# Four early x loads, single-tile norms, more warm-up products and one last FFN group of four tiles

## The chip, the cores and the metric

The kernel runs on one core of one Trainium2 chip. The metric is the device time of one execution in microseconds. A core has five instruction queues that matter here: TensorE (PE, with its weight loads, PEld), VectorE (DVE), ScalarE (ACT), GpSimd (POOL) and SyncE (SP), which issues nearly all DMAs. Each runs its own list of instructions in order and waits on semaphores for the others.

## The reference

One transformer block with adaptive layer norm, on x of 2048 x 512 in bf16. A vector c gives, through silu and w_mod, six vectors of 512: shift, scale and gate for each half.

```
mod = silu(c) @ w_mod                      # 6 x 512: sa, ca, ga, sb, cb, gb
h = layernorm(x) * (1 + ca) + sa
q, k, v = split(h @ wqkv)                  # 32 heads of 16
logits[s, w] = q[s] . k[s - 2w] / 4        # w = 0..7, masked where s - 2w < 0
o[s] = sum_w softmax(logits)[s, w] * v[s - 2w]
x = x + ga * (o @ wo)
h = layernorm(x) * (1 + cb) + sb
x = x + gb * ((silu(h @ w1) * (h @ w3)) @ w2)   # inner width 1792
```

## The kernel before

The 2048 rows are 16 tiles of 128. All weights and x stay in SBUF once they are loaded. The work has three stages, and the stages of different tiles overlap.

**First norm and q, k, v.** `LN1` groups the tiles as 0-1, 2-3, 4-7, 8-11, 12-15. `ln_stats` (line 576) computes mean and variance on DVE, adds epsilon, raises to the power -1/2 on POOL, and normalizes on DVE (tile 0 on ACT). It takes one tile at a time in the first group and pairs in the others; for tiles 0 and 1 the epsilon is added on DVE, else on POOL. `ln_T` (line 644) brings h into feature-major form: PE transposes with an eviction on ACT that also applies scale and shift, or, for the groups that `DMA_T` names, DMA transposes followed by ACT. `proj_qk` and `proj_v` are PE products; ACT evicts them, and v is stored to a scratch in DRAM by SP (line 764), from which `values` later loads shifted windows of 1 MB. Three buffers hold v between eviction and store, so an eviction of v waits until an earlier store has landed.

**Attention.** `BLOCKS` takes pairs of tiles. The products of q with eight shifted k are DVE instructions of 128 x 4096 (`pq`, line 781), summed per head by PE (line 791). Softmax runs on DVE and ACT. DVE multiplies the weights into the loaded windows of v (line 868 and 873), PE adds them up (line 886), ACT evicts, a DMA transpose on SP turns the result (`ot`, line 893), PE multiplies by wo (line 901), and DVE adds the residual (line 906).

**FFN.** `FFN` groups the tiles. `ln_sums` (line 613) is the second norm, on ACT and POOL. For each of 14 slices of the inner width `ffn_unit` (line 911) makes a product with w1 (silu on ACT), one with w3, and their product on DVE (line 933); products have 256 or 512 columns by the group's size. `ffn_w2` (line 940) multiplies by w2 per tile in two halves of seven slices; tiles 14 and 15 go in column halves (line 950). A group's units may start only as slices of the group before are read, since 20 buffers serve 14 slices.

**The start.** `rows` gives the layout in which x is read (the attention uses two orders of rows). Tiles 0 to 7 go to a borrowed buffer (`sb_pq`) for the first norm and are loaded a second time, later, into `x_sb`. SP issues the loads in order: x of tile 0, of tile 1, the first 1 MB of w_mod (`wm_s`, line 451), and then slices of wqkv and x. Until w_mod has landed, PE runs `NWARM` warm-up products of 256 columns (line 545), the small product that transposes c, and the transposes of tile 0. Then follow the modulation products (line 531), the modulated h on DVE and ACT, and the first q and k products (line 728).

**The order.** Nothing is scheduled at run time: `ORDER` lists all operations by their number in the order of construction, and each engine's queue is that list cut down to its own operations (`place`, line 143). `SLOTS` gives the buffer of every pooled value. `synchronize` (line 165) puts a wait where a value or a buffer comes from another engine. So every queue, the one of SP with its DMAs too, is fixed and blocks at its head.

Of the kernel before, what the change touches and what calls it, by code (L numbers as in the profile page):

```python
# [264 lines left out]
FFN = [[0,1],[2,3],[4,5,6,7],[8,9,10,11],[12,13],[14,15]]  # L265
BLOCKS = [[[0, 1]], [[2, 3]], [[4, 5]], [[6, 7]], [[8, 9]], [[10, 11]], [[12, 13], [14, 15]]]
NWARM = 25
NATL = (0, 1, 2, 3, 6, 7)
NAT = (6, 7)
TURN_DMA = (4,5,6,7)  # L270
UPA = {}
DMA_T = ((3, 4), (2, 3, 4, 5))
# [3 lines left out]
def _build(p, A_x, A_wqkv, A_wo, B_w1, B_w3, B_w2, c, w_mod, out):  # L276
# [176 lines left out]
    load_x(2, 4, 30)  # L453
# [122 lines left out]
    def ln_stats(Ts):  # L576
# [10 lines left out]
        if i < 2:  # L587
            o = p.op("dve", lambda e: e.tensor_scalar(rsn, mv[:, i:i + n, 1], EPS, None, op0=ALU.add), 65, k, r=vms, w=[va])
            if i == 0:
                vneg = Val("nmean0")  # L590
                p.op("pool", lambda e: e.tensor_scalar(nb[:, 0:1, 0], mv[:, 0:1, 0], -1.0, None, op0=ALU.mult), 210, k, r=vms, w=[vneg])
        else:
            o = p.op("pool", lambda e: e.tensor_tensor(rsn, mv[:, i:i + n, 1], bass.AP(cst, 0, [[2, P], [0, n]]), ALU.add), 210, k,
                     r=vms + [vcst], w=[va])
# [46 lines left out]
    def pairs(Ts):  # L641
        return [Ts[i:i + 2] for i in range(0, len(Ts), 2)]
# [336 lines left out]
    for gi, Ts in enumerate(LN1):  # L979
        vns = [v for pr in ([[T] for T in Ts] if gi == 0 else pairs(Ts)) for v in ln_stats(pr)]  # L980
# [153 lines left out]
```

## Time and profile before

| what | value |
|---|---|
| time, median of 3 runs | 238.24 us (237.93 to 238.61) |
| the profiled execution | 237.94 us, its span 236.2 us |
| PE busy | 229.8 us, 97% |
| DVE busy | 178.8 us, 76% |
| ACT busy | 147.7 us, 63% |
| POOL busy | 20.0 us, 8% |
| granted TensorE clock | 0.999 |
| DMA moved | 40.42 MB, mean 171 GB/s |

The profile shows one execution from its first to its last instruction. Matmuls are pipelined, so a product's length is not its step; the distance between two starts is. Some records of products are missing. DMA issues on SP appear with the time that SP needs to issue them; the transfer itself ends later, when it lands.

### The profile page before, as it was taken

The page shows a single profiled execution, that of the slowest core. Times are in us where ns is not written, and L with a number is a line of the kernel's source. Part 1 is how long each engine was busy: PE and PEld are TensorE (multiplying, and loading weights), DVE is VectorE, ACT ScalarE, POOL GpSimd, SP SyncE. Part 2 cuts the span into 40 slices and gives each one's busy share as a digit, 9 for nine tenths or more (in the row PEclk, how much of TensorE's full clock was granted, in tenths as well). Part 3 has the DMA queues.
Part 4 walks back from the last instruction along what each step waited for, and adds up shares of the span by engine and source line. Part 5 has one row for each costly group of instructions (what it writes and reads, how often), then busy time and mean ns, then how long its engine had stood idle before and what let it go on. Part 6 is the DMA issues. An engine that isn't in the chain of part 4 may idle for free.

```text
span 236.2 us, 4478 instructions
## 1 busy us (share of the span) xinstructions
PE 229.8 (97%) x1768; PEld 136.0 (58%) x1794; DVE 178.8 (76%) x286; ACT 147.7 (63%) x298; POOL 20.0 (8%) x44
## 2 busy tenths in 40 slices
PE   7999999999999999999999999999999999999995
PEld 5766554544597586564444444444465457485774
DVE  5598999999979999999999999793364403434433
ACT  3299587979989855985746786829866415040300
POOL 5432050002000000110001010001010000000000
PEclk9999999999999999999999999999999999999999
DMA  6999589999999783896591854441311000000202
GB/s 198 391 324 311 140 305 236 220 261 369 359 264 405 280 263 100 255 263 217 147 293 54 305 139 69 86 180 44 76 38 44 25 0 1 0 25 0 71 0 89
DMA packets 42717, 40.42 MB, mean 171 GB/s; under 512 B 23224, under 2 KB 39624, under 8 KB 40648
## 3 DMA queue, kind: packets, MB, share of 16 engines
q1 hardware_dynamic: 42688, 40.14, 57.4%
q8 instruction: 14, 0.23, 0.4%
q14 instruction: 7, 0.06, 0.1%
q10 hardware_dynamic: 8, 0.00, 0.0%
HBM read 30.67 MB, written 4.21 MB: 148 GB/s over the span
## 4 chain that ended last, share of the span: by engine, by line
PE 87%; DMA 4%; ACT 4%; DVE 1%; issue 1%; SPq 1%; POOL 0%; ACTq 0%
PE pall L918 41%; PE pall L962 18%; PE pall L728 7%; PE pall L901 5%; PE pall L750 4%; PE pall L886 3%; PE pall L791 3%; PE pall L950 3%; DMA sb_wm_s<-in_w_mod_dram 2%; DMA v_scratch_dram<-sb_v 2%; PE pall L671 1%; SPq L124 1%; ACT sb_xn L636 1%; ACT sb_xn L621 1%; ACT sb_q L739 1%
## 5 line engine op out<-in xcount | busy, mean ns | idle before, releaser
L918 PE MATMUL pall<-sb_h,sb_w 128*128 128x256 bf16 (+1 forms) x664 | 101.1, 307 | 0.6 <-ACT sb_ac L892 0.2
L918 PEld LDWEIGHTS pall<-sb_h,sb_w 128*128 128x128 bf16 x672 | 65.0, 98 | 35.8 <-issue 1.1
L933 DVE TENSOR_TENSOR sb_hh<-sb_sg,pall 128x256 bf16<-128x256 bf16 (+1 forms) x84 | 39.9, 506 | 36.7 <-PE pall L918 31.2
L924 ACT ACTIVATE sb_sg<-pall 128x256 bf16<-128x256 f32 (+1 forms) x84 | 36.0, 452 | 45.3 <-PE pall L918 41.9
L962 PE MATMUL pall<-sb_w,sb_hh 128*128 128x512 bf16 x190 | 44.0, 379 | 0.3
L781 DVE TENSOR_TENSOR sb_pq<-sb_q,sb_kT 128x4096 bf16<-128x4096 bf16 x16 | 36.4, 2285 | 0.0
L962 PEld LDWEIGHTS pall<-sb_w,sb_hh 128*128 128x128 bf16 x196 | 18.9, 98 | 21.7 <-issue 0.4
L728 PE MATMUL pall<-sb_h,sb_wqkv 128*128 128x512 bf16 (+1 forms) x156 | 30.3, 335 | 0.7 <-issue 0.4
L728 PEld LDWEIGHTS pall<-sb_h,sb_wqkv 128*128 128x128 bf16 x160 | 14.7, 98 | 11.9 <-ACT sb_v L760 0.8
L972 DVE TENSOR_TENSOR sb_o<-pall,sb_x 128x512 bf16<-128x512 f32 (+1 forms) x18 | 11.1, 628 | 9.7 <-PE pall L962 6.0
L629 POOL TENSOR_TENSOR sb_rs<-sb_rs,sb_cst 128x2 f32<-128x2 f32 x8 | 6.8, 855 | 135.4 <-ACT sb_rs L627 135.4
L656 ACT ACTIVATE sb_h<-sb_h,sb_modc 128x512 bf16<-128x512 bf16 (+1 forms) x24 | 16.3, 733 | 3.0 <-DMA sb_h<-sb_xn 3.0
L868 DVE TENSOR_TENSOR sb_vsh<-sb_vsh,sb_al 128x4096 bf16<-128x4096 bf16 x7 | 15.9, 2287 | 0.0
L750 PE MATMUL pall<-sb_wqkv,sb_h 128*128 128x512 bf16 x60 | 15.2, 379 | 0.3 <-issue 0.2
L901 PE MATMUL pall<-sb_wo,sb_ot 128*128 128x512 bf16 x60 | 14.7, 379 | 0.3 <-issue 0.2
L873 DVE TENSOR_TENSOR sb_vsh<-sb_vsh,sb_al 128x2048 bf16<-128x2048 bf16 x12 | 14.3, 1222 | 0.3 <-DMA sb_vsh<-v_scratch_dram 0.2
L892 ACT ACTIVATE sb_ac<-pall 128x512 bf16<-128x512 f32 x16 | 9.6, 604 | 5.7 <-PE pall L886 5.6
L679 ACT ACTIVATE sb_h<-pall,sb_modc 128x256 bf16<-128x256 bf16 (+1 forms) x18 | 9.8, 614 | 4.7 <-DVE sb_modc L536 3.8
L636 ACT ACTIVATE sb_xn<-sb_x,sb_nb,sb_rs 128x512 bf16<-128x512 bf16 x16 | 12.6, 807 | 0.1
L906 DVE SCALAR_TENSOR_TENSOR sb_x<-pall,sb_x 128x512 bf16<-128x512 f32 x16 | 10.9, 687 | 1.6 <-PE pall L901 1.5
L621 ACT ACTIVATE sb_xn<-sb_x,sb_nm 128x512 bf16<-128x512 bf16 x16 | 11.4, 715 | 0.2
L740 ACT ACTIVATE sb_kT<-pall 128x512 bf16<-128x512 f32 x16 | 9.4, 604 | 3.1 <-PE pall L728 3.1
(94 smaller groups left out, 212.7 us busy)
## 6 DMA issues: line engine op xcount, KB each, us to landing
sb_vsh<-v_scratch_dram SPq DMA_DIRECT2D x13, 1024.0 KB, 7.2
sb_w<-in_B_w_dram SPq DMA_DIRECT2D x6, 512.0 KB, 6.6
sb_vshx<-v_scratch_dram SPq DMA_DIRECT2D x3, 1024.0 KB, 6.5
sb_w<-in_B_w_dram SPq DMA_DIRECT2D x6, 384.0 KB, 6.3
sb_x<-in_A_x_dram SPq DMA_DIRECT2D x8, 256.0 KB, 6.9
v_scratch_dram<-sb_v SPq DMA_DIRECT2D x16, 128.0 KB, 6.2
out_dram<-sb_o SPq DMA_DIRECT2D x14, 128.0 KB, 2.3
sb_wqkv<-in_A_wqkv_dram SPq DMA_DIRECT2D x6, 256.0 KB, 6.3
```

The costliest lines, as they stand in the source:

```text
L636: p.op("act", lambda e, vn=vn, T=T: e.activation(vn.at[:], x_sb[:, T, :], ACT.Identity, bias=nb[:, T, :], scale=rs[:, NT + T, :]), c_act(5 ...
L656: return e.activation(vh.at[:, ft, 0:n * P], vh.at[:, ft, 0:n * P], ACT.Identity, bias=modc[:, 8 * which + ft:8 * which + ft + 1], scale=m ...
L728: ins = e.matmul(bank(vp)[:, j * n:(j + 1) * n], wqkv[:, t, col:col + P], vh.at[:, t, 0:n], start=(t == ORDER[0] and j == 0), stop=(t == O ...
L750: ins = e.matmul(bank(vp), vh.at[:, t, tt * P:(tt + 1) * P], wqkv[:, t, 2 * D:3 * D], start=(t == ORDER[0]), stop=(t == ORDER[-1]))
L781: return e.tensor_tensor(vp.at[:], in0, in1, ALU.mult)
L868: return e.tensor_tensor(v_w, v_w, a_w, ALU.mult)
L873: return e.tensor_tensor(v_w, v_w, a_w, ALU.mult)
L901: ins = e.matmul(bank(vy), bass.AP(vt.at, ft * 2 * P + a, [[KT * 2 * P, P], [step_, P]]), wo[:, ft, :], start=(ft == 0), stop=(ft == KT - 1))
L918: ins = e.matmul(bank(vp)[:, 0:n], wt[:, t, fi * P:(fi + 1) * P], vh.at[:, t, 0:n], start=(t == 0), stop=(t == KT - 1))
L924: p.op("act", lambda e: e.activation(vt.at[:, 0:n], bank(vgp)[:, 0:n], ACT.Silu), c_act(n), k, r=[vgp], w=[vt], table="silu")
L933: p.op("dve", lambda e: e.tensor_tensor(vh_.at[:, 0:n], vt.at[:, 0:n], bank(vup)[:, 0:n], ALU.mult), c_dve(n), k, r=[vt, vup], w=[vh_])
L962: ins = e.matmul(bank(vz), vhh[fi].at[:, tt * P:(tt + 1) * P], w2[:, fi, :], start=(fi == 0), stop=(fi == NF - 1))
```

## The change

Four things are edited in the source.

- x of tiles 2 and 3 is loaded by two loads of 128 KB in place of one of 256 KB.
- `ln_stats` takes tiles 2 and 3 one at a time too, and adds epsilon for them on DVE.
- `NWARM` is 30 in place of 25.
- The last two FFN groups, tiles 12-13 and 14-15, become one of four tiles. Its transposes stay DMA transposes, and tiles 14 and 15 keep their column halves of w2.

All operations are renumbered, and `ORDER` and `SLOTS` are new. Read as queues, the new order differs as follows.

- SP: the loads of x go out as tile 2, 3, 0, 1, all ahead of w_mod's first part; the slices of wqkv follow without x between the first and the second. The second load of x2 and x3 comes right behind that of x14 and x15, ahead of the first store of v (before: behind the second pair of 1 MB windows). That of x4 and x5 comes ahead of the small store of zeros (before: behind the transposes of tiles 8 to 11). That of x6 and x7 comes behind the first slice of w1 (before: behind the first transpose of tile 10). One half of the second part of w_mod comes behind the transposes of tiles 8 to 11 (before: ahead of the first store of v). The transposes of tiles 12 to 15 go out ahead of the store of tile 4's v and of a part of wo, and not behind them.
- DVE: statistics of tiles 2 and 3 come ahead of those of 0 and 1; tiles 2 and 3 are normalized right behind the first h. The columns of both gates are cast one behind the other, ahead of tile 10's normalization (before: the second one behind tile 8's).
- POOL: the long select for the mask comes behind the powers of tiles 8 to 11 (before: ahead of those of 2 and 3).
- PE: 27 warm products ahead of tile 0's transposes and three behind them. Among the transposes of tiles 4 to 7, v of tile 3 stands behind the first two of the pair of feature blocks that ACT evicts first, and that pair goes ahead of the other. The first gate's products come between the two last q products of tiles 2 and 3, the second gate's right behind them. From there on the order is nearly the same up to the last wo product; then the units of tiles 8 to 11 are finished in order, and those of tiles 12 to 15 follow, six units, the first half of w2 of tiles 8 to 11, seven units, the second half, one unit, and then w2 of tiles 12 to 15.
- ACT: k of tiles 12 to 15, its first block, is evicted ahead of the first sums of the second norm (before: behind them). The silus of the last two groups follow PE's order, with the four modulations of tiles 12 to 15 ahead of three of them.

```diff
-FFN = [[0,1],[2,3],[4,5,6,7],[8,9,10,11],[12,13],[14,15]]
+FFN = [[0, 1], [2, 3], [4, 5, 6, 7], [8, 9, 10, 11], [12, 13, 14, 15]]
-NWARM = 25
+NWARM = 30
-DMA_T = ((3, 4), (2, 3, 4, 5))
+DMA_T = ((3, 4), (2, 3, 4))
...
     p.dma(wm_s[0][:], wm_view[:, :, 0:1024], ("load", 2), (512, 2048), w=[vwms[0]])
     load_wqk(0)
-    load_x(2, 4, 30)
+    for T in range(2, 4):
+        p.dma(x_in(T), rows(x2d, T, plain=NATL), ("load", 31 + T), (128, 1024), r=x_hold if T in early else [], w=[vxl[T]])
     load_wqk(1)
...
-        if i < 2:
+        if i < 4:
             o = p.op("dve", lambda e: e.tensor_scalar(rsn, mv[:, i:i + n, 1], EPS, None, op0=ALU.add), 65, k, r=vms, w=[va])
...
-        vns = [v for pr in ([[T] for T in Ts] if gi == 0 else pairs(Ts)) for v in ln_stats(pr)]
+        vns = [v for pr in ([[T] for T in Ts] if gi < 2 else pairs(Ts)) for v in ln_stats(pr)]
...
 ORDER = [
-    21, 20, 8, 0, 9, 18, 66, 22, 10, 11, 3, 67, 12, 4, 1, 68, 13, 23, 19, 69, 2, 70, 16, 24, 17, 71, 5, 72, 6, 62, 75,
+    25, 20, 8, 0, 9, 18, 67, 26, 10, 11, 3, 68, 12, 4, 1, 69, 13, 21, 19, 70, 2, 71, 16, 22, 17, 72, 5, 73, 6, 63, 23,
...
```

More of the change, by code (lines that the diff above doesn't have):

```diff
@@ L262, in c_dve @@
     return 60 + n * 137 // 128
-FFN = [[0,1],[2,3],[4,5,6,7],[8,9,10,11],[12,13],[14,15]]
+FFN = [[0, 1], [2, 3], [4, 5, 6, 7], [8, 9, 10, 11], [12, 13, 14, 15]]
 BLOCKS = [[[0, 1]], [[2, 3]], [[4, 5]], [[6, 7]], [[8, 9]], [[10, 11]], [[12, 13], [14, 15]]]
-NWARM = 25
+NWARM = 30
 NATL = (0, 1, 2, 3, 6, 7)
 NAT = (6, 7)
-TURN_DMA = (4,5,6,7)
+TURN_DMA = (4, 5, 6, 7)
 UPA = {}
-DMA_T = ((3, 4), (2, 3, 4, 5))
+DMA_T = ((3, 4), (2, 3, 4))
 LN1 = [[0, 1], [2, 3], [4, 5, 6, 7], [8, 9, 10, 11], [12, 13, 14, 15]]
```

131 rows, old and new, of tables (ORDER, SLOTS) are left out of this document.

## The prediction

> **What bounds the kernel now.** I read the page first, then the chain of waits, then busy time by stretch, then the timeline of single engines around each edit.
>
> ```profile
> span 236.2 us, 4478 instructions
> PE 229.8 (97%) x1768; PEld 136.0 (58%) x1794; DVE 178.8 (76%) x286; ACT 147.7 (63%) x298; POOL 20.0 (8%) x44
> PE 87%; DMA 4%; ACT 4%; DVE 1%; issue 1%; SPq 1%; POOL 0%; ACTq 0%
> ...
> 1.69 5.80 DMA sb_wm_s<-in_w_mod_dram
> ...
> 47.14 4.26 DMA v_scratch_dram<-sb_v
> 51.42 0.60 ACT sb_v L760
> ...
> 136.02 6.04 PE pall L918 x28
> ...
> 206.52 6.11 PE pall L918 x56
> ```
>
> The last rows are pieces of the chain: start, length, what. The kernel is one long PE queue. Only two things stand ahead of it or in it: the first load of w_mod, which lands at 1.69 + 5.80 = 7.49, and a detour between 47 and 59, where a store of v, an ACT eviction and the second layer norm of tiles 0 and 1 decide. The price of a step on PE is read here too: 6.11 / 56 = 0.109 us for 256 columns, 6.04 / 28 = 0.216 for 512.
>
> ```profile
> 21.50:67.00 45.50, 44.42 (x410) 23.36 (x415) 44.51 (x51) 38.31 (x76) 4.85 (x5) 1.00 0.97 270
> 68.50:151.50 83.00, 82.15 (x640) 46.73 (x649) 81.71 (x114) 61.50 (x125) 3.85 (x5) 1.00 0.68 210
> ```
>
> Columns: stretch, length, busy PE, PEld, DVE, ACT, POOL, granted clock, DMA share, GB/s. From 21.5 to 67 DVE is busy 44.5 of 45.5 us and the DMA engines 0.97. PE runs level with a full DVE and a full DMA queue there; whatever starts DVE or SP later in that stretch can reach PE.
>
> **The start: two more loads ahead of w_mod.**
>
> ```profile
> 0.78 0.86 SPq L124 DMA_DIRECT2D sb_pq<-in_A_x_dram  x2
> ...
> 1.24 2.31 PE L545 MATMUL pall<-sb_ones 128*128 128x256 bf16 x10 [1.24 <-DVE sb_ones L387]
> ...
> 3.21 0.68 DVE L582 BATCH_NORM_STATS2 sb_st<-sb_pq 128x6 f32<-128x512 bf16 x1
> ...
> 6.13 0.36 PEld L671 LDWEIGHTS pall<-sb_ident,sb_xn 128*128 128x128 bf16 x4 [0.28 <-ACT sb_xn L603]
> ...
> 6.55 0.74 PE L545 MATMUL pall<-sb_ones 128*128 128x256 bf16 x3
> ...
> 8.60 3.39 PE L728 MATMUL pall<-sb_h,sb_wqkv 128*128 128x256 bf16 x28
> ...
> 12.35 0.34 PEld L671 LDWEIGHTS pall<-sb_ident,sb_xn 128*128 128x128 bf16 x6 [0.21 <-DVE sb_xn L607]
> ...
> 2.00:3.00 1.00, 1.00 (x7) 0.67 (x5) 0.00 (x0) 0.96 (x2) 0.86 (x6) 1.00 1.02 243
> 5.00:7.50 2.50, 2.30 (x14) 1.33 (x11) 0.79 (x3) 0.81 (x1) 2.17 (x4) 1.00 1.05 389
> ```
>
> SP puts out a load every 0.45 us (1.69 - 0.78, over two), so two more move w_mod's issue by 0.9. The 262 KB ahead of it cost 262 / 389 = 0.67 at the later rate and 262 / 243 = 1.08 at the rate of the first loads. I take 0.9, ends 0.67 and 1.08: the row of 2.00 to 3.00 is that of the same kind of load, but the issue is the slower of the two only up to 0.9. [...] The q and k weights behind it wait less: the load of x2 and x3 that stood between the first and the second of them is gone, which returns 0.67.
>
> Five more warm products fill 1.05 us: ten of them take 2.31, of which the last one's 0.42 of pipeline is not a step, so a step is 1.89 / 9 = 0.21. Tile 0 is now normalized third: two statistics go ahead of it, so it starts at 3.21 + 2 x 0.68 = 4.6 instead of 3.21, its chain of 2.9 us to PE (3.21 to 6.13) and two small DVE instructions (0.2) end at 7.8, and four transposes and three products later it is about 8.4, when w_mod lands. So this hides exactly; if tile 0 is 0.2 later, PE is too (the upper end holds it).
>
> What it buys: x2 and x3 are normalized before w_mod lands. PE's q and k products then no longer wait for weights (28 of them span 3.39 - 0.27 = 3.12 from first to last start, where 27 steps of 0.109 are 2.94: 0.17 lost) nor for tile 3 (0.20 at 12.35). PE gets **+0.9 - 0.37 = +0.53**, ends 0.3 and 0.7. One POOL instruction moves too: the 1.5 us select behind the powers of tiles 10 and 11, and POOL is busy for 20 of 236 us. POOL's and DVE's one-tile additions and powers (0.15 and 0.57 each) lie in their idle time there, and so does the split into two loads.
>
> **The order at 17 to 23.**
>
> ```profile
> 17.29 0.94 PE L671 MATMUL pall<-sb_ident,sb_xn 128*128 128x128 bf16 x14
> ...
> 18.29 0.81 PE L750 MATMUL pall<-sb_wqkv,sb_h 128*128 128x512 bf16 x3
> ...
> 18.27 2.79 ACT L679 ACTIVATE sb_h<-pall,sb_modc 128x512 bf16<-128x512 bf16 x4 [0.19 <-PE pall L671]
> 20.99 1.08 ACT L739 ACTIVATE sb_q<-pall 128x512 bf16<-128x512 f32 x2
> 21.37 0.16 DVE L564 CAST sb_gcol<-pall 128x4 bf16<-128x4 f32 x1 [0.70 <-PE pall L558]
> 22.16 2.28 DVE L781 TENSOR_TENSOR sb_pq<-sb_q,sb_kT 128x4096 bf16<-128x4096 bf16 x1
> ```
>
> The new order puts tile 3's v product (four steps, 0.86) between the transposes of tiles 4 to 7 whose evictions head ACT's queue. These transposes end at 19.1 instead of 18.1: 0.53 of PE's shift, and 0.86 less the three transposes (0.33) that now come after. ACT evicts h four times (2.79) and then q twice (1.08), so q of tiles 2 and 3 is out at 23.1 and DVE's first big product starts 1.0 later. DVE agrees on its own: the second gate's column is now cast right behind the first, and waits for 16 more products behind q; tile 10's normalization, which follows it, is 0.9 late. DVE has no hole from there to 67, so all of it moves by 1.0.
>
> **SP's queue.** It is in order, and from 23 to 53 it always has something ready. Of the reloads of x (0.6 of issue each), that of tiles 2 and 3 moves ahead of the first store of v and that of 6 and 7 behind w1, so one less stands between tile 10's transposes and ot.
>
> ```profile
> 31.96 1.12 SPq L124 DMA_DIRECT2D v_scratch_dram<-sb_v  x2
> 33.12 0.60 SPq L124 DMA_DIRECT2D sb_wo<-in_A_wo_dram  x1
> 33.77 7.56 SPq L124 DMA_TRANSPOSE sb_h<-sb_xn  x4
> ...
> 43.94 2.53 SPq L124 DMA_TRANSPOSE sb_ot<-sb_ac  x2
> ...
> 33.38 0.32 DVE L607 TENSOR_SCALAR sb_xn<-sb_x,sb_mv,sb_rs 128x512 bf16<-128x512 bf16 x1
> ...
> 48.19 1.89 PE L901 MATMUL pall<-sb_wo,sb_ot 128*128 128x512 bf16 x8
> DMA to landing us min/median/max: 2.7/3.1/3.4
> ```
>
> The transposes of tiles 12 to 15 go out at 33.77, just as tile 15 is normalized (33.38 + 0.32). In the new order a store of v and a load of wo, 1.1 us of issue, come behind these transposes instead of ahead. SP will stand at them from about 33.0 (before: 33.77, less the two issues, plus 0.4 from the same lateness of DVE at tile 8), until DVE delivers tile 15 at 33.70 + 1.0. So they start 0.9 later than now, and 1.1 of issue is still to be done after them. Queued behind are ot of tile 0 and 1, then w3 and the store of v that the chain goes through at 47.14. The second ot goes out at 45.2 now and lands 2.7 later, at 47.9; PE's first wo product follows at once (48.19, of which one step is not recorded). There is no slack: PE would come 0.9 + 1.1 = 2.0 late. Against it: the four transposes took 7.56 where the two of ot took 2.53, so 2.5 us is back-pressure of a full DMA queue, and 1.7 us of silence ahead of them drains some. If all that is given back, the queue is early and PE keeps its own 0.53. Between 0.53 and 2.0 I take **1.2**: the nearest row, the 7.56, stood behind the same two megabyte loads that still stand there. It takes the place of the 0.53, and does not add to it.
>
> **From 49 to 59 PE loses time already.**
>
> ```profile
> 49.92 1.89 PE L728 MATMUL pall<-sb_h,sb_wqkv 128*128 128x512 bf16 x8
> 52.08 2.76 PE L728 MATMUL pall<-sb_h,sb_wqkv 128*128 128x512 bf16 x12 [0.27 <-ACT sb_v L760]
> ...
> 58.35 0.89 PE L671 MATMUL pall<-sb_ident,sb_xn 128*128 128x128 bf16 x8
> 59.44 0.81 PE L728 MATMUL pall<-sb_h,sb_wqkv 128*128 128x512 bf16 x3 [0.20 <-issue]
> ```
>
> Eight steps from 49.92 end at 51.65, the next starts at 52.08: 0.43. Eight transposes (0.44) and one unrecorded product (0.22) from 58.35 end at 59.0, the next starts at 59.44: 0.43. Together 0.86. They could absorb a late PE, but the store of v that they wait for is behind the same queue and moves with it, so I count nothing. From 67 on, DVE's hole of 1.5 us between the two stretches above takes in its own lateness, and PE carries its 1.2 to the end.
>
> **The last four tiles as one group.** The 224 steps of 256 columns become 112 of 512: 224 x 0.109 - 112 x 0.216 = **-0.27**.
>
> ```profile
> L933 DVE TENSOR_TENSOR sb_hh<-sb_sg,pall 128x512 bf16<-128x512 bf16 x28 | 18.5, 682 | 9.1 <-PE pall L918 7.7 <-ACT sb_sg L924 1.3
> L924 ACT ACTIVATE sb_sg<-pall 128x512 bf16<-128x512 f32 x28 | 16.0, 593 | 11.5 <-PE pall L918 8.7 <-DVE sb_hh L933 2.8
> ...
> 171.98 0.20 ACT L617 ACTIVATE sb_nm<-sb_sx 128x2 f32<-128x2 f32 x1 [1.55 <-DVE sb_x L906]
> DMA to landing us min/median/max: 2.3/2.4/2.4
> ```
>
> The first two rows are groups of equal instructions: ACT needs 0.59 and DVE 0.68 for a unit of 512 columns, PE 8 x 0.216 = 1.73, so both stay covered. The group now waits for tiles 14 and 15. From the end of the last wo product at 171.2 PE has 16 half units of the group before, 13.8 us, until 185.0. The norm starts at 171.98; its ACT queue holds a silu that needs PE's seventh half unit (177.3), so the last tile is normalized at 178.8, its transpose lands 2.4 later, and four modulations, about as long as the four evictions of 2.79 above, end at 184.1. It hides by 0.9; if that cover goes, PE waits for the difference.
>
> **The sum**: +1.2 - 0.27 = +0.9 on the profiled execution, whose own time is 237.94 (236.2 and 1.7 around it). The three runs shown have 237.93 to 238.61, median 238.24; the profiled one is 0.3 below, so I forecast 237.94 + 0.9 + 0.3, **239.1**.
>
> **Rivals.** (1) SP's queue catches up: the drained DMA queue returns the back-pressure, ot lands in time, the store of v too. PE then has +0.53, some of it absorbed in the 0.86, and -0.27: from 237.6 to 238.5. For it: 7.56 against 2 x 2.53. Against: the two loads of 1 MB are still in front. It decides once the four transposes take under 6.1 us (1.5 of the 2.0 given back). (2) Faster: w_mod is only 0.67 late, PE's 0.3 is absorbed, both losses of 0.43 vanish because w3 and the store get ahead, and the merge pays: 0.3 - 0.86 - 0.27 = -0.8, 237.4. It decides only if v's store leaves SP before 46.7. (3) The merged group's norm comes late, by a further 1 us when the last transposes wait for stores ahead of them: 240.1. (4) The clock: warm products step 0.21, the q products from 8.60 on 0.109. PE now has a hole of some 0.6 us before tile 0's transposes; the slow steps lasted from 1.24 past 6.55, over 5.3 us; if that had to be served once more from tile 0's transposes at 7.8 on, q and k would run at half speed from 9.5 to 13.1 and cost 1.8: 240.3 and more. Against it: the wait of 0.3 for w_mod at 7.2 left the clock alone. [...]
>
> **Chances.** Forecast 0.50 (238.7 to 239.9 by its own ends), rival 1 0.30, rival 2 0.12, rival 3 0.05, rival 4 0.03. What can be told from no change is about 0.3%, 0.7 us. Below 237.5 lie rival 2 and the edge of rival 1, 0.13; above 238.95 four fifths of the forecast and rivals 3 and 4, 0.48; between them 0.39. The range 237.6 to 240.1 leaves out most of rival 2 and the tops of 3 and 4.
>
> **What would show it.** w_mod lands at 8.4 and the first q product starts at 9.5; the wait on tile 3's norm is gone; DVE's first 4096-wide product starts at 23.2; SP idles before the transposes of tiles 12 to 15; wo's first product comes at 49.4; the last group's units step 0.216 with no hole ahead of them. I am wrong if wo starts before 48.6 or if the losses at 52 and 59 are gone.

## The result and the profile after

| | before | after |
|---|---|---|
| median of 15 runs each | 238.61 us (237.23 to 240.92) | 241.73 us (239.15 to 243.24) |
| ratio after / before, 95% interval | | 1.0093 (1.0065 to 1.0121) |
| the profiled execution, its span | 237.94 us, 236.2 us | 240.11 us, 238.4 us |

The change makes the kernel slower by 0.93%, 2.2 us (1.6 to 2.9). The profiled executions differ by 2.2 us too; the medians differ by 3.1, since the ratio, here and below, leaves out executions over 1.5% above the fastest of the same kernel, four of the 15 of after and one of before. Forecast were 239.1 us and +0.9: the direction was right, the size was not, and 241.73 lies outside the range of 237.6 to 240.1.

The page of after, its first lines and the shares of the chain of waits by engine:

```profile
span 238.4 us, 4262 instructions
PE 232.1 (97%) x1687; PEld 125.1 (52%) x1687; DVE 177.5 (74%) x274; ACT 144.8 (61%) x280; POOL 20.3 (9%) x44
...
PE 85%; DMA 5%; ACT 5%; SPq 2%; DVE 1%; issue 0%; ACTq 0%
```

PE is at 97% as before, with 81 products fewer on record (the merge takes out 112; some products are missing from each trace). In the chain PE's share falls from 87% to 85%, and DMA and SP's queue grow from 4% and 1% to 5% and 2%: the loss is in what PE waits for. The timeline of PE in the kernel after (start, length, what, idle time before it and what ended it):

```profile
8.53 0.35 PE L532 MATMUL pall<-sb_csT_bf,sb_wm_s 128*128 128x1 bf16 x8 [0.47 <-DMA sb_wm_s<-in_w_mod_dram]
...
9.60 3.01 PE L729 MATMUL pall<-sb_h,sb_wqkv 128*128 128x256 bf16 x26
...
15.28 1.91 PE L729 MATMUL pall<-sb_h,sb_wqkv 128*128 128x256 bf16 x16
...
34.60 0.94 PE L515 MATMUL pall<-sb_csT_bf,sb_wm_s 128*128 128x1 bf16 x32
...
48.39 1.04 PE L729 MATMUL pall<-sb_h,sb_wqkv 128*128 128x512 bf16 x4
50.40 1.89 PE L902 MATMUL pall<-sb_wo,sb_ot 128*128 128x512 bf16 x8 [0.97 <-DVE sb_mx L804]
...
54.30 2.76 PE L729 MATMUL pall<-sb_h,sb_wqkv 128*128 128x512 bf16 x12 [0.28 <-ACT sb_v L761]
...
173.49 24.34 PE L919 MATMUL pall<-sb_h,sb_w 128*128 128x512 bf16 x112
...
229.60 6.28 PE L951 MATMUL pall<-sb_w,sb_hh 128*128 128x256 bf16 x56
```

Four things are to be seen in it. The start goes as forecast: w_mod is used at 8.53, the first q product stands at 9.60, and the group that was at 14.67 is at 15.28, +0.61. The four products from 48.39 on end at 49.25 (4 x 0.216), so PE itself is 1.06 late there; then it stands until 50.40, 2.21 later than the 48.19 of before. From there on the distance stays (54.30 against 52.08: 2.22). The tail gives something back. The two rows of before that answer to the last two:

```profile
171.05 16.63 PE L918 MATMUL pall<-sb_h,sb_w 128*128 128x512 bf16 x98
...
227.45 6.28 PE L950 MATMUL pall<-sb_w,sb_hh 128*128 128x256 bf16 x56
```

227.45 - 171.05 = 56.40 before, 229.60 - 173.49 = 56.11 after: 0.29 saved, 0.27 was forecast, and no hole stands ahead of the merged group.

So the whole loss is there at 50. SP's queue in the kernel after:

```profile
30.19 0.58 SPq L124 DMA_DIRECT2D sb_wm_s<-in_w_mod_dram  x1
30.90 0.89 SPq L124 DMA_DIRECT2D sb_vsh<-v_scratch_dram  x2
...
34.87 7.50 SPq L124 DMA_TRANSPOSE sb_h<-sb_xn  x4
...
46.27 2.69 SPq L124 DMA_TRANSPOSE sb_ot<-sb_ac  x2
```

The transposes of tiles 12 to 15 start 1.1 late (34.87 against 33.77; 0.9 was forecast), and they still take 7.50 us. With the store and the part of wo behind them the first transpose of ot goes out at 46.27, 2.33 later than the 43.94 of before. The second goes out at 47.69 and lands 2.5 later, at 50.15, and PE's wo follows. The row at 50.40 names DVE at line 804, but the product needs nothing of that; of what it needs, ot came last. DVE's scaling of the wo weights, which the product needs as well, had been held up too, by the last load of wo in the same queue:

```profile
48.33 1.23 DVE L988 TENSOR_TENSOR sb_wo<-sb_wo,sb_ga_bc 128x2048 bf16<-128x2048 bf16 x1 [0.82 <-DMA sb_wo<-in_A_wo_dram]
```

It ends at 49.56, so with ot alone in time PE would still have stood until then. Ahead of the four transposes go the two windows of v, 1 MB each. First before, then after; the first row has the first and the last start, the second the time from issue to landing (of two, the larger is the second window's):

```profile
L124 SPq DMA_DIRECT2D sb_vsh<-v_scratch_dram x2: 422/468/513, 29.8 to 30.3; - x2
...
DMA to landing us min/median/max: 5.0/6.5/8.0
```

```profile
L124 SPq DMA_DIRECT2D sb_vsh<-v_scratch_dram x2: 411/422/432, 30.9 to 31.4; - x2
...
  DVE sb_vsh L869: 0.3, 1
...
DMA to landing us min/median/max: 6.0/7.7/9.4
```

The second window lands at 30.3 + 8.0 = 38.3 before and at 31.4 + 9.4 = 40.8 after: 2.5 late, of which only 1.1 is a late issue. For the other 1.4 the row at 30.19 above is the candidate, and e7 below tests it: 512 KB of w_mod (one half of its second part) now go out just ahead of the windows, where x of tiles 4 and 5, 256 KB, stood before. DVE now waits for the window (0.3), and the third of the four transposes does not leave SP until about when it lands (it stands from 37.55 to 40.48, the window lands at 40.8).

### The profile page after: what moved, and what is told of

It reads as the page before. It is cut to its first block, busy times and chain, and to the rows that moved or that the text cites. A ratio compares the mean times of both kernels' runs of the same rounds, so it can differ in the third digit from the quotient of the medians.

```text
span 238.4 us, 4262 instructions
## 1 busy us (share of the span) xinstructions
PE 232.1 (97%) x1687; PEld 125.1 (52%) x1687; DVE 177.5 (74%) x274; ACT 144.8 (61%) x280; POOL 20.3 (9%) x44
## 3 DMA queue, kind: packets, MB, share of 16 engines
HBM read 30.67 MB, written 4.21 MB: 146 GB/s over the span
## 4 chain that ended last, share of the span: by engine, by line
PE 85%; DMA 5%; ACT 5%; SPq 2%; DVE 1%; issue 0%; ACTq 0%
PE pall L919 41%; PE pall L963 18%; PE pall L729 7%; PE pall L902 5%; PE pall L751 4%; PE pall L887 3%; DMA v_scratch_dram<-sb_v 3%; PE pall L792 3%; PE pall L951 3%; DMA sb_wm_s<-in_w_mod_dram 2%; SPq L124 2%; ACT sb_q L740 1%; PE pall L672 1%; DVE sb_vsh L869 1%; ACT sb_xn L622 1%; ACT sb_xn L637 1%
## 5 line engine op out<-in xcount | busy, mean ns | idle before, releaser
L919 PE MATMUL pall<-sb_h,sb_w 128*128 128x512 bf16 (+1 forms) x560 | 101.3, 337 | 0.0
L919 PEld LDWEIGHTS pall<-sb_h,sb_w 128*128 128x128 bf16 x560 | 54.1, 98 | 45.5 <-issue 0.8
L934 DVE TENSOR_TENSOR sb_hh<-sb_sg,pall 128x512 bf16<-128x512 bf16 (+1 forms) x70 | 38.1, 574 | 34.9 <-PE pall L919 30.9
L925 ACT ACTIVATE sb_sg<-pall 128x512 bf16<-128x512 f32 (+1 forms) x70 | 34.0, 508 | 37.4 <-PE pall L919 35.0
L963 PE MATMUL pall<-sb_w,sb_hh 128*128 128x512 bf16 x196 | 44.6, 379 | 0.0
L729 PE MATMUL pall<-sb_h,sb_wqkv 128*128 128x512 bf16 (+1 forms) x160 | 31.0, 337 | 0.3 <-ACT sb_v L761 0.3
L657 ACT ACTIVATE sb_h<-sb_h,sb_modc 128x512 bf16<-128x512 bf16 x20 | 15.0, 808 | 4.3 <-DMA sb_h<-sb_xn 4.3
L902 PE MATMUL pall<-sb_wo,sb_ot 128*128 128x512 bf16 x64 | 15.6, 379 | 1.0 <-DVE sb_mx L804 1.0
L751 PE MATMUL pall<-sb_wqkv,sb_h 128*128 128x512 bf16 x64 | 16.1, 380 | 0.0
```

The source lines that it names most:

```text
L657: return e.activation(vh.at[:, ft, 0:n * P], vh.at[:, ft, 0:n * P], ACT.Identity, bias=modc[:, 8 * which + ft:8 * which + ft + 1], scale=m ...
L729: ins = e.matmul(bank(vp)[:, j * n:(j + 1) * n], wqkv[:, t, col:col + P], vh.at[:, t, 0:n], start=(t == ORDER[0] and j == 0), stop=(t == O ...
L751: ins = e.matmul(bank(vp), vh.at[:, t, tt * P:(tt + 1) * P], wqkv[:, t, 2 * D:3 * D], start=(t == ORDER[0]), stop=(t == ORDER[-1]))
L902: ins = e.matmul(bank(vy), bass.AP(vt.at, ft * 2 * P + a, [[KT * 2 * P, P], [step_, P]]), wo[:, ft, :], start=(ft == 0), stop=(ft == KT - 1))
L919: ins = e.matmul(bank(vp)[:, 0:n], wt[:, t, fi * P:(fi + 1) * P], vh.at[:, t, 0:n], start=(t == 0), stop=(t == KT - 1))
L925: p.op("act", lambda e: e.activation(vt.at[:, 0:n], bank(vgp)[:, 0:n], ACT.Silu), c_act(n), k, r=[vgp], w=[vt], table="silu")
```

## The experiments

Orders are written as queues: each line is an operation of the engine named, minus and plus are where it leaves and where it goes. Every run computes the whole reference. "wo" is the start of PE's first wo product, "window" the landing of v's second window, both from the profiled execution (48.2 and 38.3 before, 50.4 and 40.8 after).

| run | edit | ratio to before (95%) | span | wo | window |
|---|---|---|---|---|---|
| e1_merge | before, last group merged | 1.0020 (0.9998 to 1.0041) | 236.5 | 48.6 | 38.9 |
| e5_merge_tail | the same, other buffers | 1.0053 (1.0023 to 1.0084) | 238.2 | 49.1 | 40.6 |
| e9_merge_own | the same, buffers of after | 1.0007 (0.9974 to 1.0040) | 239.4 | 51.3 | 42.1 |
| e2_startmerge | after, order of before from 13 us on | 1.0092 (1.0051 to 1.0132) | 240.5 | 52.0 | 43.5 |
| e6_order_merge | after, start of before | 1.0029 (0.9990 to 1.0068) | 237.2 | 49.1 | 38.8 |
| e3_sp | after, store of v and wo ahead | 1.0090 (1.0055 to 1.0125) | 240.2 | 51.7 | 43.2 |
| e4_both | e3, and PE's order at 17 to 27 | 1.0152 (1.0119 to 1.0184) | 240.9 | 52.9 | 41.2 |
| e7_wmod_early | after, w_mod's half early | 1.0010 (0.9975 to 1.0044) | 237.1 | 49.2 | 38.3 |
| e8_swap_before | before, w_mod's half late | 1.0018 (0.9985 to 1.0051) | 236.7 | 49.2 | 38.9 |
| e10_order_wearly | e6 with w_mod's half early | 0.9986 (0.9957 to 1.0015) | 236.2 | 48.6 | 37.9 |
| e11_x_early | before, x of 4 and 5 early | 0.9969 (0.9938 to 1.0000) | 235.6 | 47.8 | 37.7 |
| e12_x_early_merge | e11 and the merge | 0.9964 (0.9932 to 0.9995) | 235.9 | 48.5 | 38.5 |

**The merge alone (e1, e5, e9).** FFN and DMA_T are edited as in the change, and everything up to the last wo product keeps the order of before.

```diff
-FFN = [[0,1],[2,3],[4,5,6,7],[8,9,10,11],[12,13],[14,15]]
+FFN = [[0, 1], [2, 3], [4, 5, 6, 7], [8, 9, 10, 11], [12, 13, 14, 15]]
```

> The kernel before with only its last four tiles as one FFN group; everything up to the last wo product keeps the order of before. Theory (the merge is worth its steps, and the loss is all ahead of it): PE's first wo product stays at 48.2, the stretch from the end of the last wo product to the last column-half product shortens by 0.27 to 0.29 (224 steps of 0.109 become 112 of 0.216), span 235.9. Rival (the merged group only pays because PE came 2.2 us late, and its norm comes too late when PE is early): a hole of up to 1 us ahead of the first unit of tiles 12 to 15, span 236.2 to 236.9.

> The kernel before with its last four tiles as one FFN group, as in the first run of this kind, but with the buffers of the last group as the kernel after has them (there, other buffers added three small waits of 0.05 to 0.15 us). Theory (the merge is worth its steps): from the first unit after the last wo product to the first column-half product 56.1 us in place of 56.4, span 235.9. Rival (the group's norm is late when PE comes early): a hole ahead of a unit of tiles 12 to 15, span 236.2 or more.

> The kernel before with its last four tiles as one FFN group, the buffers from the middle of the kernel on as the kernel after has them, so that neither of the waits for buffers of the two runs before arises (0.3 us in all in the first, 1.2 us in the second). Theory (the merge is worth its steps): from the first unit after the last wo product to the first column-half product 56.1 us in place of 56.4; span 235.9 where all ahead of it goes as in the profile of before. Rival: other waits, 56.4 or more.

The tail of e9, and from e1 the row at wo:

```profile
174.52 24.34 PE L918 MATMUL pall<-sb_h,sb_w 128*128 128x512 bf16 x112
...
230.64 6.28 PE L950 MATMUL pall<-sb_w,sb_hh 128*128 128x256 bf16 x56
```

```profile
48.57 1.67 PE L901 MATMUL pall<-sb_wo,sb_ot 128*128 128x512 bf16 x7 [0.39 <-DMA sb_ot<-sb_ac]
```

With the buffers of after the stretch is 230.64 - 174.52 = 56.12, as forecast. The buffers chosen for e1 and e5 added waits of 0.3 and 1.2 us, so these two say little of the merge; e9's profiled execution was 3 us late by then, since w_mod came late and the clock fell (last section), and its ratio shows no loss. The merge is worth 0.28 to 0.29 in the traces of e9 and after, less than a comparison here can tell. These three runs teach something beside: up to 170 us their queues are those of before, and yet wo stood at 48.6, 49.1 and 51.3, and the second window took 8.6, 9.7 and 9.1 us to land (8.0 before). One profile is one draw of this.

**The start and the order taken apart (e2, e6).** e2 is the kernel after with all queues between 13 us and the last wo product in the order of before. e6 is its complement: the new order, but w_mod behind x of tiles 0 and 1, and 25 warm products.

```diff
 e2 against after, SP, up to the windows (behind them SP and the other engines likewise; h1, h2: the halves of w_mod's second part; x again: second load):
-x14-15, x2-3 again, store v0, v2, x4-5 again, zeros, h1, transpose 10, store v1, transposes 11, 9, 8, h2, windows 0, 1
+zeros, h2, store v0, x14-15, store v2, h1, transpose 10, x6-7 again, store v1, transposes 11, 9, 8, x4-5 again, windows 0, 1
 e6 against after, SP:
-x2, x3, x0, x1, first 1 MB of w_mod, wqkv slices 1, 2, 3, 4
+x0, x1, first 1 MB of w_mod, wqkv slice 1, x2 and x3, slices 2, 3, 4
```

> The kernel after with every queue between 13 us and the last wo product put back in the order of before; the new start (two loads ahead of w_mod, single-tile norms, 30 warm products) and the merged group stay. Theory (the loss comes from the order at 17 to 23 and on SP's queue, and the later start is taken up): the first q product at 9.6, wo's first product between 48.2 and 48.8, span 236.0 to 236.6. Rival (the 0.6 by which the start makes PE late runs on and grows through DVE): wo's first product at 49.0 or later, span 236.9 or more.

> The kernel before with the new order of all queues from 13 us on and the merged group, but with the start of before (w_mod behind x of tiles 0 and 1, 25 warm products). Theory (the second 1 MB window of v decides: DVE's second weighted product and SP's third transpose both wait for it, and the new order puts 512 KB of w_mod ahead of it): the second window lands at 39.6 to 40.4 in place of 38.3, wo's first product at 49.2 to 49.8, span 237.0 to 237.6. Rival (the late start makes the whole loss, the order nothing): wo's first product at 48.2 to 48.5, span 236.0 to 236.3.

In e2 the theory fails: wo stands at 52.0. The rival's bound (49.0 or later) holds, but not in the way it gave. The start of the profiled execution:

```profile
9.19 0.35 PE L532 MATMUL pall<-sb_csT_bf,sb_wm_s 128*128 128x1 bf16 x8 [1.15 <-DMA sb_wm_s<-in_w_mod_dram]
...
10.41 4.21 PE L729 MATMUL pall<-sb_h,sb_wqkv 128*128 128x256 bf16 x26
```

w_mod came 0.7 later than in the profile of after, and the first 26 products took 4.21 in place of 3.01: the granted clock was 0.75 from 9 to 10 us and 0.50 from 10 to 12 (last section). PE was 2.6 late at 15 us, the window landed at 43.5, and wo was 3.8 late. The clock is not all of it: five of e2's eight executions ran at a mean clock of 1.000 and took 239.5 to 241.7 us (another, unexplained, took 346 us at a mean clock of 0.658). e6 comes close to its theory at wo (49.1 for 49.2 to 49.8, PE waiting 1.1 ahead of it), but with the window at 38.8, and not at 39.6 to 40.4. So the old order does not save the kernel once the start is late, although e2 has h2 early, as before; why it loses as much as after is not shown. e6's interval holds no change.

**SP's issue times (e3, e4).**

```diff
 SP, e3 (e4 has PE's and DVE's order at 17 to 27 of before as well):
 second store of the three ahead of the transposes (v of tile 3)
+store of tile 4's v
+wo, second part
 transposes of tiles 15, 12, 14, 13
-store of tile 4's v
-wo, second part
```

> The kernel after with one change in SP's queue: the store of tile 4's v and the load of a part of wo go out ahead of the transposes of tiles 12 to 15 again. Theory (SP's issue time sets ot): the two issues of 0.6 fall into SP's idle stretch at 33.7, the transposes still start at 34.9, ot leaves 1.2 earlier, wo's first product at 49.3 in place of 50.4, span 237.3. Rival (the DMA queue sets it: the transposes cannot leave before the 1 MB windows have landed at 40.8, and 640 KB more in front of them only lengthen their 7.5 us): wo's first product stays at 50.2 to 50.6, span 238.2 to 238.5.

> The kernel of the run before (store of v and load of wo ahead of the transposes of tiles 12 to 15) and in addition PE's and DVE's order at 17 to 27 as before the change: v of tile 3 behind the transposes of tiles 4 to 7, both last q products ahead of the first gate, the second gate and its cast later. Theory: DVE's first 4096-wide product starts at 22.7 (0.6 from the start alone), tile 15 is normalized 0.5 to 1.0 earlier, wo's first product at 48.4 to 48.8, span 236.3 to 236.7. Rival (the DMA queue): the windows are issued 0.5 to 1.0 earlier and so are all behind them, wo at 49.5, span 237.4.

SP's queue in e3, and what waited for its windows:

```profile
29.97 0.58 SPq L124 DMA_DIRECT2D sb_wm_s<-in_w_mod_dram  x1
30.69 0.89 SPq L124 DMA_DIRECT2D sb_vsh<-v_scratch_dram  x2
...
34.89 10.16 SPq L124 DMA_TRANSPOSE sb_h<-sb_xn  x4
...
47.68 2.53 SPq L124 DMA_TRANSPOSE sb_ot<-sb_ac  x2
```

```profile
L124 SPq DMA_DIRECT2D sb_vsh<-v_scratch_dram x2: 410/421/432, 30.7 to 31.1; - x2
...
  DVE sb_vsh L869: 2.8, 1
...
DMA to landing us min/median/max: 6.8/9.4/12.1
```

The transposes start where they did (34.89), two issues fewer stand behind them, and ot still goes out 1.4 later than in after: the four take 10.16, while the second window takes 12.1 us to land (31.1 + 12.1 = 43.2). The theory that the order of the issues sets ot falls; the ratio is that of the whole change. Its rival misses as well (wo at 51.7 for 50.2 to 50.6): PE stood 1.86 us for DVE's product with the late window, and wo followed PE's own products. (Why the window takes 12.1 here and 9.4 in after, with only 256 KB more queued behind it, is not explained.) In e4 nothing is regained either. Its PE and the granted clock (the third column from the right) around 34:

```profile
34.98 0.94 PE L515 MATMUL pall<-sb_csT_bf,sb_wm_s 128*128 128x1 bf16 x32 [1.38 <-issue]
...
37.14 3.08 PE L729 MATMUL pall<-sb_h,sb_wqkv 128*128 128x512 bf16 x8
```

```profile
35.00:36.00 1.00, 0.92 (x33) 0.88 (x35) 1.00 (x4) 0.49 (x1) 0.00 (x0) 1.00 0.99 418
36.00:37.00 1.00, 1.00 (x3) 0.39 (x3) 1.00 (x3) 0.00 (x0) 0.00 (x0) 0.56 1.09 442
37.00:38.00 1.00, 1.00 (x4) 0.31 (x3) 1.00 (x2) 0.00 (x0) 0.00 (x0) 0.50 1.09 344
```

L515 is the product that reads that half of w_mod. The trace names no releaser for it, but the load's landing does:

```profile
L124 SPq DMA_DIRECT2D sb_wm_s<-in_w_mod_dram x1: 581/581/581, 30.7 to 30.7; - x1
...
DMA to landing us min/median/max: 4.2/4.2/4.2
```

30.7 + 4.2 = 34.9, and the product starts at 34.98. PE stands 1.4 us for it and then runs at a granted clock of 0.50: eight products take 3.08 where eight took 1.89. Five of e4's six executions, this one among them, had a mean clock of 0.992 or 0.993. In e3 the same wait is 0.83 (landed 35.0, started 35.10), in the profile of after 0.14 (landed 34.5, started 34.60).

**One DMA (e7, e8).** Both readings point at the 512 KB at 30.19: the windows land behind them, and PE waits for them. e7 moves this one DMA in the kernel after; in e8 it changes places with x of tiles 4 and 5 in the kernel before.

```diff
 e7, SP:
 x of tiles 2 and 3, second load
+w_mod, second part, one half
 store of tile 0's v
 ...
 transposes of tiles 10, 11, 9, 8
-w_mod, second part, one half
 windows of v, 0 and 1
 e8, SP:
-h2, store v0, ..., transposes 11, 9, 8, x4-5 again, windows 0, 1
+x4-5 again, store v0, ..., transposes 11, 9, 8, h2, windows 0, 1
```

> The kernel after with one DMA moved: the half of w_mod's second part (512 KB) that goes out just ahead of the two windows of v goes out ahead of the first store of v again. Theory (the second window of v decides): it lands at 39.3 to 39.8 in place of 40.8, DVE does not wait for it, SP's third transpose leaves 1.0 earlier, wo's first product at 49.2 to 49.6, span 237.3. Rival (SP's issue times, or the late start): the window may land earlier, wo's first product stays at 50.1 to 50.6, span 238.2 to 238.5.

> The kernel before with two DMAs changing places in SP's queue: the half of w_mod's second part (512 KB) goes out just ahead of the windows of v, and x of tiles 4 and 5 (256 KB) ahead of the first store of v. Theory (the second window of v decides, and has little slack): it lands 0.7 to 1.1 later, at 39.0 to 39.4, the third transpose and ot leave as much later, wo's first product at 48.9 to 49.3, span 236.9 to 237.3. Rival (there is slack): wo's first product at 48.2, span 236.2.

e7, its windows, SP's queue and PE:

```profile
L124 SPq DMA_DIRECT2D sb_vsh<-v_scratch_dram x2: 432/464/495, 30.3 to 30.9; - x2
...
DMA to landing us min/median/max: 4.7/6.1/7.4
```

```profile
30.32 0.97 SPq L124 DMA_DIRECT2D sb_vsh<-v_scratch_dram  x2
...
35.25 5.91 SPq L124 DMA_TRANSPOSE sb_h<-sb_xn  x4
...
45.06 2.54 SPq L124 DMA_TRANSPOSE sb_ot<-sb_ac  x2
```

```profile
48.37 1.04 PE L729 MATMUL pall<-sb_h,sb_wqkv 128*128 128x512 bf16 x4
49.24 1.89 PE L902 MATMUL pall<-sb_wo,sb_ot 128*128 128x512 bf16 x8
```

The second window lands at 30.9 + 7.4 = 38.3. The transposes start even later than in after and take 5.91 in place of 7.50, with the store of v and the part of wo still behind them. wo follows PE's own products without a wait, at 49.24, and the ratio falls from 1.0093 to 1.0010; the two intervals do not meet. In the kernel after, this one DMA is most of the loss. It is so in that kernel: the same move is worth 0.8% with the late start (after and e7) and 0.4% with the start of before (e6, 1.0029, and e10 below, 0.9986, whose intervals overlap), so most of the loss needs both; why they add to more than their parts is not shown. In e8 the window is only 0.6 later, and the loss sits where the half itself is read:

```profile
32.96 0.95 PE L514 MATMUL pall<-sb_csT_bf,sb_wm_s 128*128 128x1 bf16 x32 [0.89 <-DMA sb_wm_s<-in_w_mod_dram]
```

PE is 1.0 late from there to wo (49.2 for 48.2) and 0.5 late at the end (span 236.7 for 236.2). The rival (there is slack) is wrong in this profile, the theory wrong as to the place; the ratio tells neither from no change. It says too little here: 7 of e8's 12 executions had a mean clock of 0.993 or 0.986, against 2 of 35 of before beside them, and the median of all its executions is 240.40 against 239.03. So the late half probably costs the kernel before something too, in the clock; the wait for it is on record in the profiled execution alone.

**What the start costs (e10).** e10 has the new order, the merge and this half early, but the start of before.

```diff
 e10 against e7, SP:
-x2, x3, x0, x1, first 1 MB of w_mod, wqkv slices 1, 2, 3, 4
+x0, x1, first 1 MB of w_mod, wqkv slice 1, x2 and x3, slices 2, 3, 4
```

> The kernel after without its new start (w_mod behind x of tiles 0 and 1, 25 warm products) and with the 512 KB half of w_mod ahead of the first store of v; the new order and the merged group stay. Against the run with the new start and this half moved, it shows what the start costs. Theory (the start makes PE 0.8 to 1.0 late and all of it reaches the end once nothing else waits): PE's first wo product at 48.1 to 48.4, span 235.9 to 236.3, so 0.8 to 1.2 less than with the new start. Rival (PE waits for ot there anyway and the start is free): wo's first product at 49.1, span 237.0.

```profile
48.59 1.89 PE L901 MATMUL pall<-sb_wo,sb_ot 128*128 128x512 bf16 x8
...
227.47 6.28 PE L950 MATMUL pall<-sb_w,sb_hh 128*128 128x256 bf16 x56
```

PE's last stage begins at 227.47, in e7 at 228.30: the late start is worth 0.83 there in the profiles (0.65 at wo, 48.59 against 49.24), and nothing later takes it up. The ratios (0.9986 and 1.0010) agree with that and cannot prove it. PE's and DVE's new order costs nothing that the ratio shows; in the profile wo is 0.40 later than before, at 48.59 where the theory had 48.1 to 48.4, and that is within the scatter of single profiles (48.6 in e1, whose queues are those of before).

**Less ahead of the windows (e11, e12).** If the windows pace that stretch, less ahead of them should help the kernel before as well.

```diff
 e11, SP (e12 has the merge as well):
 x of tiles 6 and 7, second load
+x of tiles 4 and 5, second load
 store of tile 1's v
 transposes of tiles 11, 9, 8
-x of tiles 4 and 5, second load
 windows of v, 0 and 1
```

> The kernel before with one DMA moved the other way: x of tiles 4 and 5 (256 KB), which goes out just ahead of the windows of v, goes out behind x of tiles 6 and 7, 6 us earlier, where the DMA engines are half idle. Theory (the second window's landing paces SP's queue): the windows leave 0.6 earlier, the second lands at 37.0 to 37.6 in place of 38.3, ot lands 0.7 earlier, PE's two losses of 0.43 at 52 and 59 shrink, span 235.4 to 236.0, and the median 0.3 to 0.8 below that of before. Rival (PE, not the queue, sets the pace there): no change.

> The two runs before this in one: x of tiles 4 and 5 earlier and the last four tiles as one group, in the order of before. If both are worth what they should be: span 235.1 to 235.7, the median 0.6 to 1.1 below that of before. Rival: the median as before or above it.

In e11 the window lands 0.6 earlier and wo starts at 47.8, in e12 0.2 later and at 48.5; e12's profile gains the merge's 0.28 and nothing else. Both medians are 0.9 to 1.0 us below that of before in the same comparison (237.87 and 237.95 against 238.83). Only e12's interval, 0.9932 to 0.9995, lies wholly below 1, and narrowly, one of twelve intervals here. So e12 is probably a little faster than before, by up to 0.7%; its profile does not show where that would come from.

## Why the prediction was wrong in size

Step by step, as it was put:

- **The start: right as to the trace, wrong as to where it ends.** w_mod landed at 8.48 (8.4), the first q product at 9.60 (9.5), the waits on weights and on tile 3's norm are gone (26 products in 3.01), and PE had +0.61 (+0.53). But the forecast let a later wait take its place, and with that wait away e7 starts its last stage 0.83 later than e10. That w_mod's landing itself scatters (8.5 after, 9.1 in e2) was left out.
- **The order at 17 to 23: right.** DVE's first 4096-wide product starts at 23.37 (23.2 forecast, 22.16 before) behind the second gate's cast:

```profile
22.59 0.16 DVE L565 CAST sb_gcol<-pall 128x4 bf16<-128x4 f32 x1 [1.33 <-PE pall L559]
...
23.37 2.28 DVE L782 TENSOR_TENSOR sb_pq<-sb_q,sb_kT 128x4096 bf16<-128x4096 bf16 x1
```

- **SP's queue: here it failed.** The term was taken as 1.2 between 0.53 and 2.0 and measured 2.21, above its upper end. It was built from SP's issue times, 0.9 of lateness and 1.1 of issues moved behind the transposes, with a rebate for a drained DMA queue; that 2.5 us of the 7.56 were back-pressure of that queue was an estimate from 7.56 against 2 x 2.53. The row at 30.19 was not in it: the front part lists that one half of w_mod goes behind the transposes of tiles 8 to 11, and the prediction gave this move no price. It puts 512 KB where 256 KB were, and the second window lands 9.4 us after its issue in place of 8.0. So the rebate was not paid: the four transposes took 7.50. In e7, without it, they took 5.91, below the 6.1 from which rival 1 was to decide, and PE alone set wo. That 256 KB more is what makes the landing late is not clean: with 256 KB just ahead it took 8.0 to 10.5 us (before, e1, e2, e5, e9), with 512 KB 8.7 to 12.1 (after, e3, e4, e6, e8), and only with nothing there 7.4 to 8.1 (e7, e10, e11, e12). The 1.1 for the issues moved behind the transposes depends on how long these take. In e10, which keeps the issues there, wo waits for nothing (48.59, behind PE's own four products from 47.72); in e7 the first transpose of ot leaves at 45.06, 1.1 later than before, while PE is 1.05 late itself; e3 takes the issues away and gains nothing.
- **Who reads a moved load was not asked.** PE's product at line 515 reads this half. In the profile of after PE waits 0.14 and is later where it is in e7 (48.39 and 48.37 at the four products ahead of wo); in e3, e4 and e8 it waits 0.8 to 1.4 there. How much of the 3.1 us between the medians comes from this wait, and how much from the window, was not separated.
- **The two losses of 0.43: right.** They stayed (0.45 before 54.30, of which the row shows 0.28 as a wait on v's eviction, and 0.44 after the eight transposes that now start at 60.70), and count nothing.
- **The merge: right**, 0.29 for 0.27 (the factors as printed give 0.22, unrounded ones 0.28), and rival 3 did not come.
- **The clock: hidden in the profiled execution, not in all.** Rival 4 named the price, 1.8, and gave it 3 in 100; both were estimates. Three of the 15 executions of after had a mean granted clock of 0.993, by which I estimate 0.7% of 240, 1.7 us. Of the executions of before in the experiments, 5 of 89 had such a clock. The place was not the one named alone: e2 lost it at w_mod, e4 at line 515.
- **The last 0.3, from the profile to the median, was too small.** For after it is 241.73 - 240.11 = 1.62 (before, over its 15 runs, 0.67). That is half of the miss of 2.6; how much of it is the clock, the wait at line 515 or scatter stays open.

The sum in the profiles: +2.21 at wo, +0.2 more by 170 us, -0.29 in the tail, +2.2 in all; +1.2 - 0.27 was forecast.

## What to carry to other kernels

Price every DMA that changes its place twice: by who reads it, and by what lands behind it; a load that is only listed as moved is an unpriced term. Where a large transfer stands in a queue of DMAs, the sum has to carry its landing and not issue times alone: here the second window landed 2.5 us late, of which 1.1 was a late issue. Before an order is rearranged by hand, look for a small load that can leave its place ahead of such a transfer: here e11 and e12, which move one load of 256 KB, are the only versions whose medians lie 0.9 us or more under that of before.

## What the runs showed of the hardware

- **The clock fell at pauses of 1.15 to 1.43 us, and not at every pause.** In e9's profiled execution w_mod was late, with the start of before:

```profile
8.47 0.35 PE L531 MATMUL pall<-sb_csT_bf,sb_wm_s 128*128 128x1 bf16 x8 [1.43 <-DMA sb_wm_s<-in_w_mod_dram]
...
9.54 4.90 PE L728 MATMUL pall<-sb_h,sb_wqkv 128*128 128x256 bf16 x28
```

```profile
9.00:10.00 1.00, 1.00 (x29) 0.94 (x25) 0.95 (x6) 0.31 (x1) 0.00 (x0) 0.98 1.04 394
10.00:11.00 1.00, 1.00 (x7) 0.76 (x5) 1.00 (x2) 0.25 (x1) 0.00 (x0) 0.50 1.08 385
```

  A pause of 1.43 and then 1.07 us of one-column products, with four transposes among them, 2.5 us together, and the clock is at 0.50 for an estimated 3.4 us (from means of 0.98, 0.50, 0.50, 0.50 and 0.81 in the five microseconds from 9 to 14). e2 (1.15 and 1.2; 0.75, 0.50, 0.50 and 0.54 from 9 to 13, so the fall came within those products) and e4 (1.38 and 0.94; 0.56, 0.50, 0.50 and 0.74 from 36 to 40) show the same; 0.47 and 1.07 in after, and 0.89 and 0.95 in e8's profiled execution, left the clock at 1.00. In e3 a pause of 1.86 us before the second window's products, with none of one column behind it, left it at 1.00 too. What in such a stretch counts, the pause alone or the one-column products as well, no run isolates. 7 of the 12 executions of e8 had a mean clock of 0.993 or 0.986 and five had not; what decides that, no run here shows.
- **The landing of 1 MB scatters between executions of the same queue**: 8.0, 8.6, 9.7 and 9.1 us from issue in the kernel before and in the three with only the tail changed (e1, e5, e9). Single runs of either kernel lie 3.7 to 4.1 us apart; how much of that is this scatter, and where it comes from, stays open.
- **The four DMA transposes occupied SP for longer than ot's**: they took 5.91 us in e7, 7.50 in after, 7.56 in before and 10.16 in e3, where the two of ot took 2.5 to 2.7, and ended 1.6 to 3.0 after the second window's landing in these four. The window alone does not hold them: in after the first two took 1.25 and 1.35, about as ot's did (1.27 and 1.38), with the window still in flight, and the third took 2.93. Which of the loads ahead holds them was not separated.
